# A half-split weight load, batch 1's key features by halves of heads, and a later w2 load in a fused attention and mixer kernel

## The chip, the cores and the metric

The kernel runs on one core of a Trainium2 chip. A core has five engines that matter here: TensorE (PE in the profile, with its weight loads as PEld), VectorE (DVE), ScalarE (ACT), GpSimd (POOL) and SyncE (SP). SP and POOL issue the transfers between the device memory and the on-chip memory; sixteen DMA engines carry them. The metric is the device time of one execution in microseconds (us), and a kernel's time is the median of several executions. Before the change it is 319.8 us, the median of 5 runs (318.88 to 320.85).

## The reference

Eight batches of eight heads, 576 positions, head size 64. The first part is a linear attention with cosine weights, the second a mixer with a low-rank mix over positions and a wide layer over channels:

```python
q_p = phi(q, cos_w, sin_w)          # relu(x)*cos next to relu(x)*sin: 128 features
k_p = phi(k, cos_w, sin_w)
kv  = einsum('bhsf,bhsd->bhfd', k_p, v)
z   = k_p.sum(axis=2)
x   = (q_p @ kv) / (q_p @ z + 1e-6)  # heads side by side: [8, 576, 512]
u   = x + (x^T @ U @ V)^T            # rank 32, over positions
out = u + relu(u @ w_ch1) @ w_ch2    # 512 -> 2048 -> 512
```

The weights `w_ch1` and `w_ch2` are 4 MB each in float32. Inputs and output are float32; the kernel multiplies in bf16.

## The kernel before, in words

**Tiles.** A batch's 576 positions are five chunks: c = 0 to 3 with 128 positions each, and a tail, c = 4, with 64, which lies in the lower or upper half of the partitions for even or odd batches. `kst`, `vst`, `qst` hold a batch's main rows as loaded, `kt`, `vt`, `qt` its tails. `k_prep` and `q_prep` make features from them, one instruction for the cosine half and one for the sine half of a chunk, each on the engine that the call names (lines 228 and 230). `v_prep` and `v_block` cast v into `v_ext` (lines 103 and 105), whose 65th column is one, so that `kv_unit` (line 262) gives kv and z together, for four heads at a time. `kv_unit` runs over five chunks for each of its heads and then casts its result from the accumulator to `kv_sb`. `den_unit` (line 321) makes the denominators and `xh_unit` (line 338) the quotient x for four heads. `A_unit` and the `uTd_` functions make the low-rank part and u transposed. `g1_main` (line 491) makes 128 of the 2048 hidden columns of a batch, with four matmuls, one for each 128 rows of w1 (d = 0 to 3), and a ReLU on ACT (line 500). `g2_part` (line 543) is the second wide layer. `keep_warm` (line 179) issues matmuls on zeros, whose result nobody reads.

**Order.** The order on each engine is written out by hand: the program's order of calls is each engine's order. The first two batches have code of their own: `chain0` and `chain1`. The rest run beside the wide layers, from a plan by slots. A slot is one `g1_main`, `g1_tail` or `g2_part`; what `at(j, ...)` names runs behind slot j of the first batch's wide layer. `chain1` runs behind slot 7. Of batch 0's wide layer, columns j = 0 to 7 come before it, and j = 8 to 13 are spread through it by `fill`, starting with `g1_main(0, 8)` in `fill(1)`.

**The start.** SP issues batch 0's loads in the order q, k, tails, v, and then k and v for heads 4 to 7. POOL issues the weights, casting to bf16 on the way. To hold them back, POOL first copies one element of `vst` into `mark` (line 738), and so waits for v of heads 0 to 3; then comes w1's first quarter of columns (line 91), which j = 0 to 3 need. The second quarter, for j = 4 to 7, is issued inside `chain0`, behind POOL's casts of v for heads 4 to 7. The third and fourth quarters follow a copy that waits for `q_tlT` (line 772). w2, four loads of 512 KB as bf16 (line 97), is issued in slot 6.

`g1_main(0, j, True)` makes only the matmuls d = 0 and 1 and leaves the accumulator open. The program does so for j = 0, then closes the last two quarters of u transposed, and does j = 1 and 2 in the same way, before slot 0 finishes j = 0:

```python
chain_end(0, a0)
g1_main(0, 0, True)
uTd_close(0, 2, V_)
uTd_close(0, 3, A_)
g1_main(0, 1, True)
g1_main(0, 2, True)
```

**Batch 1.** Its q, k, v loads are issued on SP in this order behind `chain0`. Its q buffers are shared with batch 0's, so SP waits there for batch 0's last q features. Slots 4 to 6 make the key features of batch 1, for all eight heads at once, cosine on DVE and sine on ACT, between the ReLUs of j = 4 to 6. `chain1` then starts with `kv_unit(1, 0)`, heads 0 to 3; its cast is on DVE. Behind it come v's cast for heads 4 to 7 on ACT, and further down `kv_unit(1, 1)` for heads 4 to 7, with its cast on ACT. At the end of `chain1`'s first half SP writes one element of the denominators to `mark2` (line 707), and through that wait holds batch 2's loads back, which are issued behind slots 11 and 12. Batch 2's features start in slot 26.

Of the kernel before, what the change touches and what calls it, by code (L numbers as in the profile page):

```python
# [17 lines left out]
def kernel(  # L18
# [18 lines left out]
    P = 128  # L37
# [5 lines left out]
    TS = 64  # L43
# [5 lines left out]
    def tail(b):  # L49
        lo = TS * (b % 2)  # L50
        return slice(lo, lo + TS)
# [34 lines left out]
    w1_bf = const.tile([P, 4, DH], BF16)  # L86
    w2_bf = const.tile([P, NJ, DM], BF16)

    def w1_load(n):
        cs = slice(n * 512, n * 512 + 512)  # L90
        nc.gpsimd.dma_start(
            out=w1_bf[:, :, cs], in_=moe_w_ch1.rearrange("(d p) n -> p d n", p=P)[:, :, cs]
        )

    def w2_load(n):
        js = slice(n * 4, n * 4 + 4)
        nc.gpsimd.dma_start(
            out=w2_bf[:, js, :], in_=moe_w_ch2.rearrange("(j p) n -> p j n", p=P)[:, js, :]
        )

    def cast(eng, o, i):
        if eng is nc.scalar:
            nc.scalar.activation(out=o, in_=i, func=AF.Copy, bias=0.0, scale=1.0)  # L103
        else:
            eng.tensor_copy(out=o, in_=i)  # L105


    V_, A_, G_ = nc.vector, nc.scalar, nc.gpsimd
# [5 lines left out]
        out=iota[:, 0:4], pattern=[[1, 4]], base=0, channel_multiplier=4,  # L114
        allow_small_or_imprecise_dtypes=True,
    )
    for lo in (0, TS):
        nc.gpsimd.iota(
            out=iota[lo : lo + TS, 4:5], pattern=[[1, 1]], base=512, channel_multiplier=1,
# [40 lines left out]
        out=U_bf[:, 0:4, :], in_=moe_U[0:512, :].rearrange("(p c) r -> p c r", c=4)  # L160
# [20 lines left out]
    mark = const.tile([TS, 1], FP32)  # L181
# [16 lines left out]
    def V_evac(eng):  # L198
        cast(
            eng, V_bf.rearrange("p c t -> p (c t)"),  # L200
            v4_ps[0].rearrange("p a n -> p (a n)")[:, 0 : 5 * P],
        )


    k_p, q_p, q_pT, kv_sb, x_bf, A_sb = {}, {}, {}, {}, {}, {}
# [13 lines left out]
    def v_block(b, h0, h1, c0, c1, eng):  # L219
        cast(  # L220
            eng,
            v_ext[b % 2][:, c0:c1, h0:h1, 0:D].rearrange("p c h d -> p h c d"),
            vst[b][:, h0:h1, c0:c1, :],
        )
# [9 lines left out]
    def prep(dst, src, b, c, engs, h0, h1):  # L234
        rows = slice(0, P) if c < 4 else tail(b)
        for i, (w, eng) in enumerate(zip((cosw, sinw), engs)):
            if eng is not None:
                scaled_relu(
                    eng, dst[rows, h0:h1, i * D : i * D + D], src[rows], w[rows, c : c + 1]
                )  # L240

    def k_prep(b, c, engs, h0=0, h1=H):
        if b not in k_p:
            k_p[b] = pool.tile([P, 4, H, 2 * D], BF16, tag="k_p", bufs=1, name="k_p")
        src = kst[b][:, h0:h1, c, :] if c < 4 else kt[b][:, h0:h1, :]
        prep(k_p[b][:, c] if c < 4 else k_tl, src, b, c, engs, h0, h1)
# [7 lines left out]
    def kv_unit(b, hg, tag, bufs, eng=None):  # L254
        if b not in kv_sb:
            kv_sb[b] = pool.tile([P, H, E], BF16, tag="kv", bufs=2, name="kv")
        acc = ps.tile([P, 4, E], FP32, tag=tag, bufs=bufs, name="kv_ps")
        vx = v_ext[b % 2]
        for i in range(4):
            h = hg * 4 + i  # L260
            for c in range(5):
                nc.tensor.matmul(  # L262
                    out=acc[:, i, :],
                    lhsT=k_p[b][:, c, h, :] if c < 4 else k_tl[:, h, :],
                    rhs=vx[:, c, h, :],
                    start=(c == 0),
                    stop=(c == 4),
                )
        cast(eng or V_, kv_sb[b][:, hg * 4 : hg * 4 + 4, :], acc)
# [32 lines left out]
    def qT_of(b, c, h):  # L302
        return q_pT[b][:, c, h, :] if c < 4 else q_tlT[:, h, :]

    def x_alloc(b):
        if b not in x_bf:
            x_bf[b] = pool.tile([P, 4, DM], BF16, tag="x_bf", bufs=2, name="x_bf")

    def x_of(b, c, rows=slice(0, P)):
        return x_bf[b][:, c, :] if c < 4 else x_tl[rows, :]  # L310
# [21 lines left out]
    def xh_unit(b, c, h0, h1, rec, tag, bufs, eng=None):  # L332
        x_alloc(b)
        n = h1 - h0
        rows = slice(0, P) if c < 4 else tail(b)
        acc = ps.tile([P, n, D], FP32, tag=tag, bufs=bufs, name="xh_ps")
        for h in range(h0, h1):
            nc.tensor.matmul(  # L338
                out=acc[:, h - h0, :], lhsT=qT_of(b, c, h), rhs=kv_sb[b][:, h, 0:D],
                start=True, stop=True,  # L340
            )
        if eng is not None:
            for h in range(h0, h1):
                eng.activation(
                    out=x_of(b, c, rows)[:, h * D : h * D + D], in_=acc[rows, h - h0, :],
                    func=AF.Copy, bias=0.0, scale=rec[rows, c, h - h0 : h - h0 + 1],
                )
            return
        nc.vector.tensor_tensor(
            out=x_of(b, c, rows)[:, h0 * D : h1 * D].rearrange("p (i d) -> p i d", d=D),  # L350
            in0=acc[rows],
            in1=rec[rows, c, :].unsqueeze(2).to_broadcast([P if c < 4 else TS, n, D]),
            op=ALU.mult,
        )
# [232 lines left out]
    ORD = (4, 0, 1, 2, 3)  # L587
# [57 lines left out]
    O2, G3 = ("o", 2), ("g", 3)  # L645
# [11 lines left out]
    def chain0():  # L657
        v_prep(0, 0, 4, (4,), (A_,))
        v_block(0, 0, 4, 0, 3, V_)
        v_block(0, 0, 4, 3, 4, A_)  # L660
        k_prep(0, 4, (A_, A_), 4, 8)
        kv_unit(0, 0, "T", 1)
        qtr_unit(0, 4, 0, H, V_, *G3)
        keep_warm(2, "o", 2)
        for c in (0, 1):
            k_prep(0, c, (V_, A_), 4, 8)
        rec0 = den_unit(0, 0, 4, "X", 1)
        for c in (2, 3):
            k_prep(0, c, (V_, A_), 4, 8)
        v_prep(0, 4, 8, (4,), (G_,))  # L670
        v_block(0, 4, 8, 0, 2, G_)
        v_block(0, 4, 8, 2, 4, A_)
        w1_load(1)
        for n, c in enumerate(TL):
            xh_unit(0, c, 0, 4, rec0, *(O2, O2, G3, G3, G3)[n], A_ if n == 1 else None)
        keep_warm(1, "X", 1)
        kv_unit(0, 1, "T", 1, A_)
        rec1 = den_unit(0, 4, 8, "X", 1)
        a0 = A_unit(0, "T", 1, A_, 0, 256)
        for n, c in enumerate(TL[:3]):  # L680
            xh_unit(0, c, 4, 8, rec1, *(O2, O2, G3)[n])
        chain_begin(0)
        uTd_mm(0, 0)
        uTd_mm(0, 1)
        for n, c in enumerate(TL[3:]):
            xh_unit(0, c, 4, 8, rec1, *G3)
        uTd_evac(0, 0, A_)
        uTd_evac(0, 1, A_)
        keep_warm(2, "o", 2)
        return a0  # L690

    def chain1(fill):
        kv_unit(1, 0, "T", 1)
        fill(0)
        rec0 = den_unit(1, 0, 4, "X", 1)
        v_block(1, 4, 8, 0, 4, A_)
        fill(1)
        for n, c in enumerate(ORD):
            xh_unit(1, c, 0, 4, rec0, *O2)
            if n == 1:  # L700
                fill(2)
            if n == 3:
                kv_unit(1, 1, "T", 1, A_)
        fill(3)
        rec1 = den_unit(1, 4, 8, "T", 1)

        nc.sync.dma_start(out=mark2, in_=rec1[0:1, 0, 0:1])
        for c in ORD[:2]:
            xh_unit(1, c, 4, 8, rec1, *O2)
        chain_begin(1)  # L710
        a0 = A_unit(1, "T", 1, A_, 0, 256)
        for c in ORD[2:4]:
            xh_unit(1, c, 4, 8, rec1, *O2)
        fill(4)
        uTd_mm(1, 0)
        uTd_mm(1, 1)
        uTd_evac(1, 0, A_)
        uTd_evac(1, 1, A_)
        xh_unit(1, ORD[4], 4, 8, rec1, *O2)
        fill(5)  # L720
        chain_end(1, a0)
# [7 lines left out]
        if c in (1, 3):  # L729
            keep_warm(1, "X", 1)  # L730
    V_four("X", 1)
    V_evac(V_)
    for c in TL:
        k_prep(0, c, (V_, A_ if c < 3 else V_), 0, 4)
    q_prep(0, 4, (V_, A_))
    keep_warm(14, "o", 2)

    G_.tensor_copy(out=mark, in_=vst[0][0:TS, 0, 0, 0:1])
    w1_load(0)
    a0 = chain0()  # L740
    alloc_q(1)
    load_main(qst[1], q, 1)
# [20 lines left out]
    def at(j, *thunks):  # L763
        beside.setdefault(j, []).extend(thunks)

    for n, c in enumerate(ORD):
        if n > 1:
            at(n - 2, lambda c=c, n=n: q_prep(1, c, (V_, A_ if n % 2 == 0 else V_)))
        tg = ("T", 1) if n % 2 else O2
        at(1 + n, lambda c=c, tg=tg: qtr_unit(1, c, eng=V_, tag=tg[0], bufs=tg[1]))  # L770
        at((4, 5, 5, 6, 6)[n], lambda c=c, n=n: k_prep(1, c, (V_, A_)))
    at(2, lambda: G_.tensor_copy(out=mark, in_=q_tlT[0:TS, 0, TS : TS + 1]))
    at(2, lambda: [w1_load(2), w1_load(3)])
    at(2, lambda: v_prep(1, 0, H, (4,), (G_,)))
    at(2, lambda: v_block(1, 0, 4, 0, 4, G_))
    at(6, lambda: [w2_load(n) for n in range(4)])
    def fill1(n):
        if n in (0, 4):
            u_unit(0, 4 if n == 0 else 0, *(O2 if n == 0 else G3))
# [67 lines left out]
```

## Time and profile before

| | before |
|---|---|
| median of 5 runs | 319.8 us (318.88 to 320.85) |
| the profiled execution | 321.33 us |
| its span, first to last instruction | 319.2 us |
| TensorE clock, mean granted | 0.995 |
| PE busy | 310.9 us (97%) |
| DVE busy | 155.9 us (49%) |
| ACT busy | 151.4 us (47%) |
| POOL busy | 35.2 us (11%) |
| w1 and w2: eight loads of 512 KB on POOL | 9.7 us to landing (median) |

The profile is one execution, recorded by the hardware. A row such as `L491 PE MATMUL g_ps<-uT,w_bf` names the line of the kernel, the engine, the operation and what it writes and reads; the bracket at the end of a row says how long the engine was idle before it and what ended the wait. The chain of work that ended last is followed back from the last instruction, at each step to what released it. Rows of stages give, for each stretch of time, the busy time of each engine with the number of instructions, the share of full speed at which TensorE's clock ran, and the DMA engines' share and rate. In them, PE busy is a modelled time: its matmuls overlap.

### The profile page before, as it was taken

The numbers are of one execution on the slowest core, as the hardware profiler recorded it, in microseconds if no ns is written. First come the engines' busy times: TensorE is split into PE (matmuls) and PEld (weight loads), VectorE is DVE, ScalarE is ACT, GpSimd is POOL, SyncE is SP. The second block draws the span as 40 slices with busy tenths as digits, with TensorE's granted clock in tenths as the row PEclk, the third lists the DMA queues.
The fourth block names the chain that finished last, engine by engine and source line by source line (L and its number), as shares of the span: only waits on it lengthen the run. The fifth ranks groups of instructions, "written<-read, shape, count | busy, mean of one in ns | idle before, by whom it ended". The sixth has DMA issues, their size and how long they took to land.

```text
span 319.2 us, 5795 instructions
## 1 busy us (share of the span) xinstructions
PE 310.9 (97%) x2380; PEld 162.8 (51%) x2380; DVE 155.9 (49%) x355; ACT 151.4 (47%) x261; POOL 35.2 (11%) x67
## 2 busy tenths in 40 slices
PE   8989899999999999999999999999999999999996
PEld 3545464476545544475455444564454444464443
DVE  8768553762877645036926585154836520001211
ACT  5838555685905256658400077559400166650000
POOL 4213400200120140000211100000121100000000
PEclk9999799999999999999999999999999999999999
DMA  8999999946185927970799459900693130001122
GB/s 230 321 256 262 200 217 330 327 134 228 48 216 146 327 74 159 245 241 2 177 252 326 169 121 228 354 10 31 139 174 101 59 91 0 2 0 68 66 87 78
DMA packets 83803, 51.82 MB, mean 162 GB/s; under 512 B 52066, under 2 KB 81026, under 8 KB 83778
## 3 DMA queue, kind: packets, MB, share of 16 engines
q1 hardware_dynamic: 76850, 40.05, 47.0%
q0 software_dynamic: 6784, 11.35, 14.7%
q8 instruction: 18, 0.29, 0.4%
q10 hardware_dynamic: 144, 0.07, 0.1%
q14 instruction: 7, 0.06, 0.1%
HBM read 36.86 MB, written 9.44 MB: 145 GB/s over the span
## 4 chain that ended last, share of the span: by engine, by line
PE 88%; DMA 6%; ACT 4%; SPq 1%; DVE 1%; issue 0%; POOL 0%; DVEq 0%; ACTq 0%
PE o_ps L543 39%; PE g_ps L491 33%; PE gt_ps L511 4%; DMA w_bf<-in_moe_w_ch_dram 3%; PE kv_ps L262 3%; PE va_ps L407 3%; PE x_ps L363 3%; DMA vst<-in_v_dram 2%; ACT hid L500 1%; PE a_ps L390 1%; PE t_ps L279 1%; ACT k_p L228 1%; ACT q_p L228 1%; SPq L81 1%; SPq L75 0%; PE xh_ps L338 0%
## 5 line engine op out<-in xcount | busy, mean ns | idle before, releaser
L500 ACT ACTIVATE hid<-g_ps 128x512 bf16<-128x512 f32 x128 | 76.2, 596 | 102.6 <-PE g_ps L491 102.2
L491 PE MATMUL g_ps<-uT,w_bf 128*128 128x512 bf16 x512 | 120.0, 382 | 0.9 <-DMA w_bf<-in_moe_w_ch_dram 0.9
L543 PE MATMUL o_ps<-w_bf,hid 128*128 128x512 bf16 (+2 forms) x528 | 119.2, 373 | 0.0
L491 PEld LDWEIGHTS <-w_bf 128*128 128x128 bf16 x512 | 49.0, 98 | 57.5 <-DMA w_bf<-in_moe_w_ch_dram 1.3
L543 PEld LDWEIGHTS <-hid 128*128 128x128 bf16 x528 | 48.7, 98 | 52.8 <-issue 1.7
L553 DVE TENSOR_TENSOR o_sb<-u_bf,o_ps 128x512 f32<-128x512 bf16 (+2 forms) x33 | 22.1, 668 | 62.7 <-PE o_ps L543 62.6
L563 POOL DMA_DIRECT2D out_dram<-o_sb x24 | 13.5, 561 | 165.8 <-DVE o_sb L553 155.8
L408 DVE TENSOR_TENSOR u_bf<-x_bf,va_ps 128x512 bf16<-128x512 bf16 x32 | 21.8, 685 | 10.1 <-PE va_ps L407 10.1
L105 DVE CAST kv<-kv_ps 128x260 bf16<-128x260 f32 x14 | 6.0, 429 | 32.0 <-PE kv_ps L262 32.0
L373 DVE TENSOR_TENSOR x_bf<-x_ps,rec 128x512 bf16<-128x512 f32 x24 | 16.6, 691 | 0.8
L228 ACT ACTIVATE q_p<-qst,sinw 128x512 bf16<-128x512 f32 (+1 forms) x24 | 15.1, 658 | 2.2 <-DMA qst<-in_q_dram 2.1
L511 PE MATMUL gt_ps<-uT_tl,w_bf 128*128 128x128 bf16 x256 | 15.6, 219 | 0.0
L407 PE MATMUL va_ps<-A_sb,V_bf 128*128 128x512 bf16 x40 | 15.2, 379 | 0.0
L543 PE MATMUL o_ps<-w_bf,hid_tl 128*128 128x512 bf16 x64 | 15.1, 379 | 0.0
L511 PEld LDWEIGHTS <-w_bf 128*128 128x128 bf16 x256 | 14.6, 98 | 0.5
L313 DVE TENSOR_SCALAR rec<-x_ps 128x8 f32<-128x8 f32 (+1 forms) x30 | 4.9, 165 | 20.2 <-PE x_ps L363 20.1
L262 PEld LDWEIGHTS <-k_p 128*128 128x128 bf16 x256 | 11.5, 97 | 5.8 <-ACT k_p L228 1.5
L230 DVE TENSOR_SCALAR k_p<-kst,cosw 128x512 bf16<-128x512 f32 (+1 forms) x31 | 14.3, 482 | 0.0
L262 PE MATMUL kv_ps<-v_ext,k_p 128*128 128x65 bf16 x256 | 12.4, 193 | 1.6 <-ACT k_p L228 0.9
L179 PE MATMUL w_ps<-zero 128*128 128x512 bf16 x35 | 11.1, 457 | 1.2 <-DVE U_bf L162 1.2
L518 ACT ACTIVATE hid_tl<-gt_ps 128x512 bf16<-128x512 f32 x16 | 9.4, 597 | 5.5 <-PE gt_ps L511 5.5
L103 ACT ACTIVATE v_ext<-vst 128x512 bf16<-128x512 f32 (+2 forms) x19 | 11.8, 636 | 0.5 <-DMA vst<-in_v_dram 0.4
(106 smaller groups left out, 252.6 us busy)
## 6 DMA issues: line engine op xcount, KB each, us to landing
qst<-in_q_dram SPq DMA_DIRECT2D x7, 1024.0 KB, 9.1
kst<-in_k_dram SPq DMA_DIRECT2D x7, 1024.0 KB, 8.1
vst<-in_v_dram SPq DMA_DIRECT2D x6, 1024.0 KB, 8.2
out_dram<-o_sb POOLq DMA_DIRECT2D x24, 256.0 KB, 2.9
w_bf<-in_moe_w_ch_dram POOLq DMA_DIRECT2D x8, 512.0 KB, 9.7
vst<-in_v_dram SPq DMA_DIRECT2D x4, 512.0 KB, 8.6
out_dram<-o_sb SPq DMA_DIRECT2D x7, 256.0 KB, 2.3
qst<-in_q_dram SPq DMA_DIRECT2D x2, 512.0 KB, 3.7
```

Source lines behind the costliest of these rows:

```text
L228: nc.scalar.activation(out=o, in_=i, func=AF.Relu, bias=0.0, scale=w)
L230: eng.tensor_scalar(out=o, in0=i, scalar1=0.0, scalar2=w, op0=ALU.max, op1=ALU.mult)
L262: nc.tensor.matmul(out=acc[:, i, :], lhsT=k_p[b][:, c, h, :] if c < 4 else k_tl[:, h, :], rhs=vx[:, c, h, :], start=(c == 0), stop=(c == 4),)
L373: nc.vector.tensor_tensor(out=x_of(b, c, rows).rearrange("p (g i d) -> p g i d", g=2, d=D), in0=view[:, :, :, 0:D], in1=rec[rows].unsqueez ...
L407: nc.tensor.matmul(out=va, lhsT=V_bf[:, c, :], rhs=A_sb[b], start=True, stop=True)
L408: nc.vector.tensor_tensor(out=u_bf[b][:, c, :] if c < 4 else u_tl[b // 2][rows, :], in0=x_of(b, c, rows), in1=va[rows, :], op=ALU.add,)
L491: nc.tensor.matmul(out=g_ps.rearrange("p (c t) -> p c t", c=4), lhsT=w1_bf[:, d, j * P : j * P + P], rhs=uT[b][:, :, d, :], start=(d == 0) ...
L500: nc.scalar.activation(out=hid[b][:, j, :], in_=g_ps, func=AF.Relu, bias=0.0, scale=1.0)
L511: nc.tensor.matmul(out=g_ps[:, jj, :], lhsT=w1_bf[:, d, j * P : j * P + P], rhs=uT_tl[pr][:, d, :], start=(d == 0), stop=(d == 3),)
L543: nc.tensor.matmul(out=o[:, cols], lhsT=lhs[:, j, c * P : c * P + P], rhs=w2_bf[:, j, cols], start=(j == 0), stop=(j == NJ - 1),)
L553: nc.vector.tensor_tensor(out=o_sb[:, cols], in0=u[:, cols], in1=o[:, cols], op=ALU.add)
L563: eng.dma_start(out=out[b, 0:512, cols].rearrange("(p c) n -> p c n", c=4)[:, c, :], in_=o_sb[:, cols],)
```

## The change

Five edits:

1. `w1_load` takes a range of 128-row blocks. The first quarter of columns is loaded as two transfers, rows of d = 0 and 1 first, d = 2 and 3 behind. Both are on POOL, one after the other.
2. w2's four loads leave slot 6. They are issued in `chain1`, behind a POOL copy that reads one element of `kv_sb[1]`, and so waits for the cast of `kv_unit(1, 0)`.
3. Batch 1's key features in slots 4 to 6 are made for heads 0 to 3 only. Those of heads 4 to 7 move into `chain1`: cosine on DVE for chunks 4, 0, 1 ahead of `kv_unit(1, 0)`, and for chunks 2, 3 behind `den_unit(1, 0..4)`; sine on ACT, all five, behind `kv_unit(1, 0)`. v's cast for heads 4 to 7 moves from behind the denominators to behind these five.
4. `V_evac`, the DVE copy of the replicated V from its accumulator, moves from ahead of batch 0's key features to behind DVE's cast of v in `chain0`.
5. In `chain0`, x of chunk 1 for heads 4 to 7 is made by four ACT instructions and not by one DVE instruction.

```diff
-    def w1_load(n):
+    def w1_load(n, d0=0, d1=4):
         cs = slice(n * 512, n * 512 + 512)
         nc.gpsimd.dma_start(
-            out=w1_bf[:, :, cs], in_=moe_w_ch1.rearrange("(d p) n -> p d n", p=P)[:, :, cs]
+            out=w1_bf[:, d0:d1, cs],
+            in_=moe_w_ch1.rearrange("(d p) n -> p d n", p=P)[:, d0:d1, cs],
         )
...
     def chain0():
         v_prep(0, 0, 4, (4,), (A_,))
         v_block(0, 0, 4, 0, 3, V_)
+        V_evac(V_)
...
-            xh_unit(0, c, 4, 8, rec1, *(O2, O2, G3)[n])
+            xh_unit(0, c, 4, 8, rec1, *(O2, O2, G3)[n], A_ if n == 1 else None)
...
     def chain1(fill):
+        for c in ORD[:3]:
+            k_prep(1, c, (V_, None), 4, 8)
         kv_unit(1, 0, "T", 1)
+        G_.tensor_copy(out=mark, in_=kv_sb[1][0:TS, 0, 0:1])
+        for n in range(4):
+            w2_load(n)
+        for c in ORD:
+            k_prep(1, c, (None, A_), 4, 8)
+        v_block(1, 4, 8, 0, 4, A_)
         fill(0)
         rec0 = den_unit(1, 0, 4, "X", 1)
-        v_block(1, 4, 8, 0, 4, A_)
+        for c in ORD[3:]:
+            k_prep(1, c, (V_, None), 4, 8)
         fill(1)
...
     V_four("X", 1)
-    V_evac(V_)
...
-    w1_load(0)
+    w1_load(0, 0, 2)
+    w1_load(0, 2, 4)
...
-        at((4, 5, 5, 6, 6)[n], lambda c=c, n=n: k_prep(1, c, (V_, A_)))
+        at((4, 5, 5, 6, 6)[n], lambda c=c: k_prep(1, c, (V_, A_), 0, 4))
...
-    at(6, lambda: [w2_load(n) for n in range(4)])
```

`ORD` is (4, 0, 1, 2, 3); `V_`, `A_`, `G_` are DVE, ACT and POOL.

## The prediction

> **What bounds the kernel now.** I read the page first: PE is busy 310.9 of 319.2 us and nothing else is over half. So time can only be won where PE stands idle or runs slowly, and the waits of PE say where: 0.9 us for a w1 transfer, 0.9 us for the key features (line 228), the rest in the first 19 us. All lie before 37 us, so I read the chain of waits there, in order of time (start, length, what):
>
> ```profile
> 12.70 0.52 POOL mark L738
> 13.21 9.72 DMA w_bf<-in_moe_w_ch_dram
> 22.98 0.61 PE g_ps L491 x2
> ...
> 28.38 1.05 PE g_ps L491 x4
> 29.46 0.60 ACT hid L500
> 30.08 0.72 ACT k_tl L228
> 30.82 0.60 ACT hid L500
> 31.44 1.33 ACT k_p L228 x2
> 32.78 0.48 ACT hid L500
> 33.26 1.23 ACT k_p L228 x2
> 34.53 0.70 PE kv_ps L262 x17
> 35.26 0.44 DVE kv L105
> ```
>
> Two things set the pace: w1's first quarter until 22.98, and ACT from 29.46, which alternates ReLUs with sine features until kv of batch 1 can run. Between them PE's weight loads show something that the chain hides:
>
> ```profile
> 22.98 0.11 PEld L491 LDWEIGHTS <-w_bf 128*128 128x128 bf16 x2 [1.12 <-DMA w_bf<-in_moe_w_ch_dram]
> ...
> 28.38 0.55 PEld L491 LDWEIGHTS <-w_bf 128*128 128x128 bf16 x4 [0.17 <-DMA w_bf<-in_moe_w_ch_dram]
> ```
>
> The second row is j = 4, the first user of w1's second quarter. That transfer was issued at 16.25 and took 12.1 us (the tile's answer for its issue), so it landed at 28.35: PE met it with hardly any slack. The rows of stages show what follows kv's wait:
>
> ```profile
> 33.00:34.00 1.00, 0.44 (x5) 0.23 (x3) 1.00 (x3) 1.00 (x3) 1.00 (x2) 1.00 1.25 209
> 34.00:35.00 1.00, 0.61 (x16) 0.49 (x17) 0.33 (x1) 1.00 (x3) 1.00 (x3) 1.00 1.25 209
> 35.00:36.00 1.00, 0.69 (x20) 0.41 (x17) 0.74 (x2) 0.93 (x1) 0.59 (x1) 1.00 1.07 154
> 36.00:37.00 1.00, 1.00 (x19) 0.59 (x16) 0.73 (x3) 0.00 (x0) 0.00 (x0) 0.76 1.23 201
> 37.00:38.00 1.00, 1.00 (x10) 0.49 (x8) 0.00 (x0) 0.10 (x1) 0.00 (x0) 0.50 1.23 199
> ```
>
> PE is 0.44 to 0.69 busy for three microseconds, then its clock (third number from the end) is 0.50 until 39.9. Four matmuls of j = 8 take 1.62 us instead of 1.03. That slow stretch is 3.4 us long and costs half of it, 1.7 us.
>
> **What the Trainium skill says.** (1) "TensorE: Matmul & The Clock Gate", Part 1: the clock falls to half when a free-running window of 3413 ns was idle, so where the window lies differs from run to run. The length agrees (36.5 to 39.9); the stretch before it was not idle, only thin, so the trace shows a wider condition. (2) "DMA: Bandwidth & Descriptors", Anatomy of one DMA: about 2 us of a POOL transfer are fixed, mostly the wait for the last byte's receipt. It agrees: the POOL queue, read by windows, has moved the first quarter's 0.52 MB by about 21.1 (packets start at 16.8, then 0.12 MB per us), and the landing is at 22.93. (3) "SBUF — State Buffer", Who interferes with whom: a DVE feature instruction with both sides in SBUF and a POOL instruction exclude each other. It agrees: of batch 1's cosine instructions, 0.47 us each, the one that meets POOL's v cast (31.50 to 32.54) takes 1.30.
>
> **Edit 1, the split.** One POOL issue more: 0.77 us, at 13.98 to 14.75. Behind it POOL casts v's tail at 14.76 and waits for v's rows until 15.68, so the second quarter is still issued at 16.25. Half of the bytes are moved at 18.8; with the same 1.9 us of receipt the first half lands at 20.7. PE is free for it at 22.03 (the end of line 442's eight matmuls), so it starts 0.95 us earlier. The second half lands where the whole did, at 22.98 to 23.3 (bounds: nothing, and a quarter microsecond if SP's loads take more of the engines). It is needed after eight matmuls of 0.216 us, at 23.76. Covered by 0.5 us; without this cover each microsecond is paid in full. But then PE reaches j = 4 at 27.43, and the second quarter, behind the same bytes in the same queue, still lands at 28.35. PE waits there for 0.95 us. Net: 0. Bounds: −0.3 if the second quarter comes early (batch 1's k tail, issued at 14.53 and 15.3 us on the way, then holds ACT instead), +0.3 if it is later by the second transfer's overhead.
>
> **Edit 3, the halves.** ACT's sine instruction takes 0.72 us for 512 columns and 0.49 for 256 (0.43 from start to start in batch 0's features). From the chain: first ReLU ends 30.06; tail half to 30.5; j = 5's matmuls end 30.73, so its ReLU ends 31.36; two halves to 32.2; ReLU to 32.75; two halves to 33.6. Before, the last ended at 34.48. kv's last 17 matmuls start 0.9 us earlier. v is no obstacle: POOL's cast ends at 32.54. DVE has three half cosines (0.27 from start to start) ahead of kv's cast: its own h 0..4 features end near 33.1, so it is free at 33.95, and kv's matmuls end at 34.3. Hidden; if DVE were late the cast would slip by the same. **−0.9.**
>
> What ACT gets back is 5 × 0.43 = 2.2 us of sines ahead of v's cast (1.07 us). Before, the ACT rows are:
>
> ```profile
> 34.86 1.07 ACT L103 ACTIVATE v_ext<-vst 128x1024 bf16<-128x1024 f32 x1
> 37.90 0.60 ACT L500 ACTIVATE hid<-g_ps 128x512 bf16<-128x512 f32 x1 [1.97 <-PE g_ps L491]
> ```
>
> so 2 us were idle there. Now: ReLU of j = 7 to 34.05, sines to 36.2, v's cast to 37.2, then the ReLU of j = 8. Queued behind are the ReLUs of j = 8 and 9; three accumulators let PE go on without them. kv for heads 4 to 7 needs v's cast: PE comes there (0.43 kv cast, 0.64 denominators, j = 8 and 9 with 0.86 each, x) at about 37.5. Covered by 0.3; bounds 0 and +0.4. On DVE the two half cosines behind the denominators end at 36.5, when the first x is wanted. 0.
>
> **The clock.** With kv 0.9 us earlier and then 0.9 us of full PE work inside the same stretch, PE's thin stretch shrinks from 3.07 (33.17 to 36.24) to 2.1 us, shorter than the 3.4 us of the slow stretch. I count the slow clock as gone: 1.7 us in this execution. Whether the timed runs had it the trace can't say: their spread, 2.0 us, is about its size. Bounds 0 and −1.7; I take 0.7 of it, because the one execution seen had it. **−1.2.**
>
> **Edit 2, w2.** POOL waits for kv's cast at 34.76; behind it on POOL are only the w2 issues and batch 2's v casts, which waited until 53.26 for data. Issue at 35.1, packets 2.6 us later as for w1's third quarter. Its 2.1 MB at the 0.205 MB per us of the rows above take 10.2 us. First use at 71.57: hidden by over 20 us. But SP's loads of batch 2 (43.70 on, 3.5 MB at 0.33) now start up to 2.6 us earlier and overlap it: 37.7 + 10.2 + 10.7 + 2 = 60.6 for the last, q, which before landed at 51.23 + 8.5 = 59.7. ACT reads it first at 63.89 − 2.6 = 61.3. Covered by 0.7; bounds 0 and +1. **0.**
>
> **Edits 4 and 5.** V's copy (0.82 us) goes into DVE's idle 0.85 us ahead of kv's cast at 14.09. The features before it end earlier, but v lands at 12.65 anyway. SP's q tail for batch 1 (12.74, waiting for these features) leaves 0.7 us earlier with k and v behind it; that is the +0.25 above. Four ACT instructions (0.90 us) fit between 19.31 and 20.29, where ACT was idle 0.98. x's tail on DVE still ends near 21.16, since PE makes it late. Both 0, bounds ±0.2.
>
> **Sum.** In the profiled execution (span 319.2, 2.1 around it, 321.33): −0.9 − 1.7 = 318.7. The median stands 1.5 below that execution, so I use the weighted clock: 319.8 − 0.9 − 1.2 = **317.7 us**.
>
> **Rivals.** *The clock stays as it was, or the timed runs never had it*: 319.8 − 0.9 = 318.9. For it: the window moves freely. Against: the thin stretch is a third shorter. *The split pays*: the second quarter also lands earlier, −0.3 more: 317.3. Against: it follows the same bytes. *A late transfer gives it back*: w1's third quarter landed at 35.2, and j = 8 now wants it at 35.3; or batch 2's q, or v's cast, each up to 1 us: 319.3. *Slower*: w1's second quarter, behind two transfers, comes later than 28.35. Each microsecond delays j = 4, the ReLUs, the sines and kv. From 3.7 us late (2.1 gained, 1.6 for half a per cent) it decides, at 321.5; POOL's 0.9 us of slack ahead of its issue speaks against it.
>
> **Numbers.** First forecast 0.55 (317.0 to 318.5), clock rival 0.2, split 0.08, late transfer 0.1, slower 0.07. Half a per cent, 1.6 us, is about what a measurement can tell from no change: below 318.2 is faster. That gives faster 0.57 (most of the first case and the split), slower 0.07, same 0.36. The range, 316.8 to 319.4, leaves out the slower case and some of the edges.
>
> **What would show it.** PE's first w1 matmul near 22.0; a wait for w1 at j = 4, near 27.4 to 28.4; kv's last matmuls from 33.6; no clock below 1.0 near 37; w2 issues near 35; no PE wait at 37.5 or 61. It is wrong if j = 4 doesn't wait, if the clock still falls, or if ACT's sines hold kv of heads 4 to 7.

## The result, and the profile after

| | before | after |
|---|---|---|
| median | 320.08 us (79 runs, 317.99 to 323.65) | 319.48 us (44 runs, 317.21 to 322.49) |
| ratio, 95% interval | | 0.998 (0.9966 to 0.9993) |
| the profiled execution | 321.33 us | 318.45 us |
| its span | 319.2 us | 316.7 us |
| TensorE clock in it, mean granted | 0.995 | 1.0 |

The ratios here leave out disturbed runs, so they are not exactly quotients of the medians. The change gains 0.6 us, a fifth of a per cent. The interval of the ratio ends below 1, but the gain is less than the half per cent that the prediction took for the least that a measurement can tell, and under a third of the forecast. The two profiled executions, though, differ by 2.9 us. The forecast for the profiled execution was 318.7, and 318.45 came; the forecast for the median was 317.7, and 319.48 came. So the trace should show the predicted steps nearly all in place, and it does; part of that agreement is luck, as is said further down.

The chain of waits of after (start, length, what):

```profile
16.16 11.54 DMA w_bf<-in_moe_w_ch_dram
...
27.75 1.04 PE g_ps L492 x4
...
30.14 0.61 ACT hid L501
30.76 0.91 ACT k_p L229 x2
31.66 0.48 ACT hid L501
32.15 0.80 ACT k_p L229 x2
...
33.00 0.70 PE kv_ps L263 x17
33.72 0.44 DVE kv L106
...
52.13 9.06 DMA qst<-in_q_dram
61.25 0.05 issue
61.30 0.72 ACT q_p L229
```

Each pair of half sines takes 0.80 to 0.91 us where the whole ones took 1.23 to 1.33, and kv's last 17 matmuls start at 33.00 instead of 34.53. 0.63 of these 1.53 us come from j = 4, which started at 27.75 instead of 28.38; 0.90 come from the halves. The stretch of the chain shown here begins with w1's second quarter, and behind it the chain has a new link: batch 2's q, at 61.

PE's weight loads of after (start, length, what; the bracket is the idle time before and what ended it):

```profile
21.73 0.15 PEld L492 LDWEIGHTS <-w_bf 128*128 128x128 bf16 x2
...
27.75 0.55 PEld L492 LDWEIGHTS <-w_bf 128*128 128x128 bf16 x4 [0.74 <-DMA w_bf<-in_moe_w_ch_dram]
...
32.99 0.10 PEld L263 LDWEIGHTS <-k_p 128*128 128x128 bf16 x1 [0.30 <-ACT k_p L229]
```

The first w1 matmul no longer waits (22.98 before, 21.73 now), and j = 4 waits 0.74 us for the second quarter: more than half of the 1.25 us won at the start is lost six microseconds on. The wait for k is down to 0.30.

The rows of stages of after (PE, PEld, DVE, ACT, POOL busy; the third number from the end is TensorE's clock):

```profile
33.00:34.00 1.00, 0.90 (x18) 0.62 (x19) 0.28 (x1) 0.97 (x3) 0.00 (x0) 1.00 1.22 203
34.00:35.00 1.00, 0.80 (x22) 0.68 (x22) 0.86 (x3) 1.00 (x3) 0.73 (x2) 1.00 1.22 209
35.00:36.00 1.00, 1.00 (x13) 0.55 (x12) 0.96 (x4) 1.00 (x3) 1.00 (x3) 1.00 0.65 89
36.00:37.00 1.00, 0.96 (x8) 0.48 (x7) 0.91 (x4) 1.00 (x3) 1.00 (x2) 1.00 0.94 53
```

PE is 0.80 busy at the least, where before it was 0.44 to 0.69, and the clock stays at 1.00. ACT, which idled 2 us there, is full: its rows of after are

```profile
33.95 1.71 ACT L229 ACTIVATE k_p<-kst,sinw 128x256 bf16<-128x256 f32 x4
35.56 1.06 ACT L104 ACTIVATE v_ext<-vst 128x1024 bf16<-128x1024 f32 x1
36.53 1.04 ACT L501 ACTIVATE hid<-g_ps 128x512 bf16<-128x512 f32 x2
```

v's cast ends at 36.6, before kv for heads 4 to 7 starts on PE at 37.14.

### The profile page after: what moved, and what is told of

Its sections match the earlier page's. It is cut to its first block, busy times and chain, and to the rows that moved or that the text cites. A ratio compares the mean times of both kernels' runs of the same rounds, so it can differ in the third digit from the quotient of the medians.

```text
span 316.7 us, 5813 instructions
## 1 busy us (share of the span) xinstructions
PE 309.5 (98%) x2380; PEld 162.5 (51%) x2380; DVE 156.2 (49%) x359; ACT 153.5 (48%) x270; POOL 36.5 (12%) x69
## 4 chain that ended last, share of the span: by engine, by line
PE 80%; DMA 8%; SPq 6%; ACT 2%; DVE 1%; issue 1%; POOL 0%; DVEq 0%; ACTq 0%
PE o_ps L544 39%; PE g_ps L492 27%; PE gt_ps L512 4%; SPq L81 4%; DMA w_bf<-in_moe_w_ch_dram 4%; DMA qst<-in_q_dram 3%; PE kv_ps L263 3%; PE x_ps L364 3%; SPq L75 2%; PE va_ps L408 2%; DMA vst<-in_v_dram 2%; PE a_ps L391 1%; ACT hid L501 1%; ACT q_p L229 1%; PE t_ps L280 1%; ACT k_p L229 1%
## 5 line engine op out<-in xcount | busy, mean ns | idle before, releaser
L492 PE MATMUL g_ps<-uT,w_bf 128*128 128x512 bf16 x512 | 118.5, 379 | 0.6 <-DMA w_bf<-in_moe_w_ch_dram 0.6
L229 ACT ACTIVATE k_p<-kst,sinw 128x256 bf16<-128x256 f32 (+1 forms) x23 | 11.9, 570 | 0.3 <-DMA kst<-in_k_dram 0.3
```

Source lines behind the costliest of these rows:

```text
L229: nc.scalar.activation(out=o, in_=i, func=AF.Relu, bias=0.0, scale=w)
L492: nc.tensor.matmul(out=g_ps.rearrange("p (c t) -> p c t", c=4), lhsT=w1_bf[:, d, j * P : j * P + P], rhs=uT[b][:, :, d, :], start=(d == 0) ...
```

## The experiments

The question was where two thirds of the forecast went. The theories: (A) the path got shorter as predicted, but the slow stretch of the clock, worth 1.2 us in the sum, was rarer before than I took it to be, or isn't gone after; (B) something behind kv gives the gain back, w2's move and batch 2's late q first of all; (C) the gain is that of the split and not of the halves.

**How the runs are read.** Each execution reports its mean granted TensorE clock. One stretch of 3.4 us at half speed in a span of 317 us makes 0.995; so an execution at 0.997 or more had no slow stretch ("full clock"). The table puts together all runs of a kernel; before's 257 are those that ran on the same chips as the four sets of experiments. Errors are standard errors; the means of two sets of the same kernel differed by up to 0.5 us, so single sets can't settle less. The full-clock runs of a kernel are those that happened to keep the clock. Where half of the runs lost it, the rest may be the ones with the shorter waits, and their mean may flatter the kernel; that is a possibility, not something shown.

| kernel | runs | mean, us | at full clock, us | with a slow stretch |
|---|---|---|---|---|
| before | 257 | 320.20 ± 0.08 | 319.58 ± 0.06 | 35% (they average 321.3) |
| after | 88 | 319.42 ± 0.12 | 319.04 ± 0.11 | 22% (they average 320.8) |
| edit 3 alone | 14 | 318.89 ± 0.24 | 318.59 ± 0.15 | 14% |
| after, w2 back in slot 6 | 58 | 319.06 ± 0.14 | 318.80 ± 0.12 | 14% |
| edits 2 and 3 | 22 | 319.45 ± 0.26 | 319.01 ± 0.22 | 23% |
| after without edit 3 | 22 | 320.11 ± 0.28 | 319.16 ± 0.19 | 45% |
| edit 1 alone | 14 | 320.11 ± 0.31 | 319.21 ± 0.16 | 50% |
| edits 4 and 5 | 22 | 320.61 ± 0.35 | 319.42 ± 0.24 | 50% |
| before, with more filler | 22 | 319.87 ± 0.18 | 319.87 ± 0.18 | none |

### Which edit gains: the halves alone, and all but the halves

Edit 3 put alone into before, and after with edit 3 undone:

```diff
     def chain1(fill):
+        for c in ORD[:3]:
+            k_prep(1, c, (V_, None), 4, 8)
         kv_unit(1, 0, "T", 1)
+        for c in ORD:
+            k_prep(1, c, (None, A_), 4, 8)
+        v_block(1, 4, 8, 0, 4, A_)
...
-        v_block(1, 4, 8, 0, 4, A_)
+        for c in ORD[3:]:
+            k_prep(1, c, (V_, None), 4, 8)
...
-        at((4, 5, 5, 6, 6)[n], lambda c=c, n=n: k_prep(1, c, (V_, A_)))
+        at((4, 5, 5, 6, 6)[n], lambda c=c: k_prep(1, c, (V_, A_), 0, 4))
```

> The kernel before with edit 3 alone: batch 1's key features by halves of heads, w2 still in slot 6, w1's first quarter whole. Theory A (the halves give 0.9 us on the path, and w2's move gives part of it back because batch 2's q lands too late): 1.0 to 1.6 us under the kernel before, so more than the whole change gives (0.6), and in the trace kv's last matmuls near 33.6, batch 2's q landing before 60. Theory B (the halves give nothing in most runs, the loads of k and v set kv): within 0.3 us of the kernel before. Theory C (the clock alone makes the difference): the mean clock of the runs rises and runs of equal clock agree with the kernel before.

> The changed kernel with edit 3 undone: key features of all eight heads in slots 4 to 6, as before; w2 still behind kv, the split and edits 4 and 5 kept. Theory A: the gain of the halves goes, so 0.0 to 0.4 us over the kernel before; kv's last matmuls near 34.5. Theory B (edit 3 gives nothing): as the changed kernel, 0.6 us under the kernel before.

Alone: 318.68 us (14 runs), ratio 0.9973 (0.9952 to 0.9994). Undone: 320.15 us (22 runs), 0.9995 (0.9973 to 1.0018). So over all runs the gain goes with the halves, and (C) falls: without them the other four edits leave 0.09 ± 0.29 us in the mean. At full clock the halves alone give 319.58 − 318.59 = 0.99 ± 0.16 us, where the prediction had 0.9. PE's weight loads with edit 3 alone:

```profile
22.91 0.11 PEld L491 LDWEIGHTS <-w_bf 128*128 128x128 bf16 x2 [1.04 <-DMA w_bf<-in_moe_w_ch_dram]
...
33.38 0.10 PEld L262 LDWEIGHTS <-k_p 128*128 128x128 bf16 x1 [0.30 <-ACT k_p L228]
```

The wait for w1 at 22.91 is untouched and the last wait for k is 0.30, as in after. With whole features the thin stretch is back, in the stages of after without edit 3:

```profile
32.00:33.00 1.00, 0.47 (x3) 0.10 (x1) 1.00 (x3) 1.00 (x3) 0.73 (x1) 1.00 1.14 246
33.00:34.00 1.00, 0.28 (x2) 0.10 (x1) 0.41 (x2) 1.00 (x2) 0.00 (x0) 1.00 1.18 249
34.00:35.00 1.00, 0.84 (x18) 0.63 (x19) 0.11 (x1) 0.59 (x2) 0.00 (x0) 1.00 1.22 231
35.00:36.00 1.00, 0.70 (x22) 0.60 (x21) 0.90 (x2) 0.08 (x1) 0.56 (x2) 1.00 1.13 189
36.00:37.00 1.00, 1.00 (x5) 0.40 (x3) 0.46 (x2) 1.00 (x1) 1.00 (x2) 0.64 0.29 51
```

and behind it, from 36.3, the slow clock.

At full clock the two tests do not agree. After without edit 3 stands at 319.16 there, 0.42 ± 0.20 us under before, and the halves add only 0.12 ± 0.22 to that; what they add in the mean, 0.69 ± 0.30, is mostly the rarer slow stretches, 22% in place of 45%. Either the twelve runs of that kernel that kept the clock are a favourable choice, or the other edits win part of the same wait that the halves win. The runs don't tell which.

### The split alone

```diff
-    w1_load(0)
+    w1_load(0, 0, 2)
+    w1_load(0, 2, 4)
```

> The kernel before with edit 1 alone, w1's first quarter in two transfers. Theory A (the gain at the first matmul is lost at j = 4, which waits for the second quarter): within 0.2 us of the kernel before; first w1 matmul near 22.0, PE idle about 0.6 to 1 us ahead of j = 4. Theory B (the split pays): 0.5 to 0.9 us under the kernel before, no wait at j = 4. Theory C (the second quarter lands later behind two transfers): over the kernel before by 0.3 us or more.

320.22 us (14 runs), ratio 1.0011 (0.9987 to 1.0036): no gain shown. (Its full-clock mean is 0.37 lower, but from seven runs only; its mean over all runs is lower by 0.09.) PE's weight loads with the split alone:

```profile
21.92 0.15 PEld L492 LDWEIGHTS <-w_bf 128*128 128x128 bf16 x2
...
27.92 0.55 PEld L492 LDWEIGHTS <-w_bf 128*128 128x128 bf16 x4 [0.74 <-DMA w_bf<-in_moe_w_ch_dram]
```

PE starts 1.06 us earlier than before and waits 0.74 at j = 4, which still starts 0.46 earlier. The rest is lost on ACT, which now waits for batch 1's k tail, where before it came to it without a wait:

```profile
30.23 0.72 ACT L229 ACTIVATE k_tl<-kt,sinw 64x512 bf16<-64x512 f32 x1 [0.63 <-DMA kt<-in_k_dram]
```

kv's last matmuls start at 34.68, against 34.53 before. The same wait, 0.73 us, stands in the profile of after without edit 3. In other executions with the split the second quarter came early enough. PE's weight loads of after with w2 in slot 6, in the first of its profiles:

```profile
26.48 0.59 PEld L492 LDWEIGHTS <-w_bf 128*128 128x128 bf16 x4
...
31.93 0.23 PEld L263 LDWEIGHTS <-k_p 128*128 128x128 bf16 x2 [0.73 <-ACT k_p L229]
32.46 0.10 PEld L263 LDWEIGHTS <-k_p 128*128 128x128 bf16 x1 [0.30 <-ACT k_p L229]
```

There j = 4 has no wait; ACT waits 0.88 us for batch 1's k tail, and PE then waits for k, 1.03 us in all. In these executions the microsecond won at the start is spent, for the most part, in front of one of these transfers or features.

### Edits 4 and 5 alone

```diff
         v_block(0, 0, 4, 0, 3, V_)
+        V_evac(V_)
...
-            xh_unit(0, c, 4, 8, rec1, *(O2, O2, G3)[n])
+            xh_unit(0, c, 4, 8, rec1, *(O2, O2, G3)[n], A_ if n == 1 else None)
```

> The kernel before with edits 4 and 5 alone: V's copy behind v's cast, x of chunk 1 for heads 4 to 7 on ACT. Both are in engines' idle times, so within 0.2 us of the kernel before at full clock (319.56), and a slow stretch in a third of the runs. Rival: DVE's earlier features let SP issue batch 1's loads earlier, which delays or hastens w1's second quarter: 0.3 us or more off.

320.19 us (22 runs), 1.0006 (0.9982 to 1.003): no difference shown, as predicted; the full-clock mean is 0.16 ± 0.25 under before's.

### The clock: filler matmuls in the thin stretch

Before, with six more matmuls on zeros ahead of `kv_unit(1, 0)`; nothing else is changed:

```diff
-    at(7, lambda: keep_warm(2, "X", 1))
+    at(7, lambda: keep_warm(8, "X", 1))
```

> The kernel before with eight instead of two matmuls on zeros ahead of chain1, which fill 1.3 us of PE's wait for kv's features. Theory A (the thin stretch at kv makes the slow clock): runs with a slow stretch fall from 37% to under 15%, and the mean by 0.3 to 0.6 us; runs at full clock stay within 0.2 us of those of the kernel before. Theory B (the slow clock comes from elsewhere): the share stays above 30% and the time within 0.2 us.

319.9 us (22 runs), ratio 0.998 (0.9958 to 1.0002). None of the 22 runs has a slow stretch, against 35% of before's. The stages of this kernel:

```profile
33.00:34.00 1.00, 1.00 (x6) 0.49 (x5) 1.00 (x3) 1.00 (x3) 0.33 (x1) 1.00 1.17 247
34.00:35.00 1.00, 0.76 (x5) 0.20 (x2) 1.00 (x1) 1.00 (x3) 1.00 (x2) 1.00 1.16 246
35.00:36.00 1.00, 1.00 (x21) 0.82 (x21) 0.16 (x1) 0.74 (x2) 1.00 (x2) 1.00 1.15 252
36.00:37.00 1.00, 0.70 (x21) 0.47 (x19) 0.96 (x2) 0.00 (x0) 1.00 (x2) 1.00 0.82 136
```

At 35%, none in 22 would come by chance about once in ten thousand times. So the thin stretch at kv is what lets the clock fall in nearly all of these runs of before, and this one edit shows it. But the filler seems to cost 0.29 ± 0.19 us at full clock, where 0.2 at most was expected, and the whole nets 0.33 ± 0.20. A slow stretch costs 321.32 − 319.58 = 1.74 us, but only in a third of the runs: 0.6 us of before's mean. That is half of the 1.2 that the forecast counted.

Filler with the halves, two more matmuls ahead of `kv_unit` and one more ahead of `den_unit`, and after with w2 in slot 6 and two more matmuls ahead of `kv_unit`:

```diff
         fill(0)
+        keep_warm(1, "X", 1)
         rec0 = den_unit(1, 0, 4, "X", 1)
...
-    at(7, lambda: keep_warm(2, "X", 1))
+    at(7, lambda: keep_warm(4, "X", 1))
```

(the line ahead of `den_unit` in the first of the two only).

> Edit 3 alone, with four instead of two matmuls on zeros ahead of chain1 and one more ahead of the denominators of heads 0 to 3. Theory A (halves 0.97 us at full clock, and the slow clock is what the thin stretch costs): no slow stretch in over 90% of the runs, 1.2 to 1.6 us under the kernel before, about 318.6. Theory B: the added matmuls delay kv, and the time is that of edit 3 alone or 0.2 to 0.4 us more.

> The changed kernel with w2 in slot 6 and four instead of two matmuls on zeros ahead of chain1: the candidate for a version better than both. If the slow clock comes from the thin stretch at kv: at most 1 run in 10 with a slow stretch, and the mean 1.3 to 1.6 us under the kernel before. If the added matmuls delay kv: full-clock mean 0.2 to 0.4 us over that of the same kernel without them.

318.86 us, 0.9978 (0.9956 to 1.0001), and 319.39 us, 0.9976 (0.9957 to 0.9995), 22 runs each. The share of slow stretches, 9% in both, can't be told from the 14% of the same kernels without filler, and the full-clock means, 319.16 and 319.25, are some 0.5 higher. The means are 0.75 and 0.89 under before's, where 1.2 to 1.6 were expected: no gain of the filler beside the halves is shown.

### The same kernel again

After unedited, in two more sets:

> The changed kernel once more, unedited, as the measure for the others of this set. So far the kernel before ran without a slow clock stretch in 37 of 59 runs, and the changed kernel in 33 of 44. If the clock is not what the change moves, again a quarter of the runs has a slow stretch, and the median is 0.5 to 0.7 us under the kernel before.

> The changed kernel once more, on the same chip as the others of this set. Full-clock mean 318.9 to 319.1, 0.4 to 0.6 us under the kernel before; a slow stretch in about a fifth of the runs.

318.89 us, 0.9965 (0.9941 to 0.9989), and 319.71 us, 0.9969 (0.9948 to 0.999), 22 runs each. The second one's profiled execution has a slow stretch, in another place. Its stages:

```profile
16.00:17.00 1.00, 0.35 (x9) 0.26 (x8) 1.00 (x4) 0.98 (x4) 0.95 (x2) 1.00 1.01 335
17.00:18.00 1.00, 0.54 (x18) 0.45 (x15) 0.52 (x2) 0.85 (x4) 0.39 (x1) 1.00 1.19 320
...
19.00:20.00 1.00, 1.00 (x17) 1.00 (x18) 0.89 (x3) 0.87 (x4) 0.00 (x0) 0.51 1.16 239
20.00:21.00 1.00, 1.00 (x8) 0.64 (x6) 0.15 (x1) 0.44 (x3) 0.00 (x0) 0.50 1.19 242
```

This is batch 0's chain, where the halves change nothing. (Edits 1, 4 and 5 do, but the share of runs with a slow stretch is the same without them: 7 of 36 with the halves and without these edits, 27 of 146 with the halves and these edits.) The profiled executions fall in line: each of the four with whole features and no added filler (before, edit 1 alone, edits 4 and 5 alone, after without edit 3) has its slow stretch between 36 and 42. Of the eleven with the halves and w2 no later than in after, seven have none, two (both with w2 in slot 6) have it between 35 and 39, and two between 19 and 24. In the two at kv, ACT had waited 0.88 and 0.78 us for batch 1's k tail. All runs of these kernels, those with added filler left out: with whole features 119 of 315 have a slow stretch (38%), with the halves 39 of 204 (19%). The halves make the clock's fall rarer, and leave other places to it.

The clock is not the only thing that changes from run to run. One execution of the kernel with w2 in slot 6 (see below; the profile of its second set) took 321.07 us without a slow stretch: batch 1's v landed late,

```profile
34.69 1.04 POOL L106 CAST v_ext<-vst 128x1024 bf16<-128x1024 f32 x1 [2.26 <-DMA vst<-in_v_dram]
```

and PE waited 2.0 us for this cast ahead of kv.

### w2's move: back to slot 6, and later still

After with edit 2 undone, three times:

```diff
     at(2, lambda: v_block(1, 0, 4, 0, 4, G_))
+    at(6, lambda: [w2_load(n) for n in range(4)])
...
         kv_unit(1, 0, "T", 1)
-        G_.tensor_copy(out=mark, in_=kv_sb[1][0:TS, 0, 0:1])
-        for n in range(4):
-            w2_load(n)
```

> The changed kernel with w2 issued in slot 6 again (edit 2 undone). Theory A (w2 behind kv overlaps batch 2's loads, and ACT waits for q near 61): 0.4 to 0.9 us under the changed kernel, 1.0 to 1.5 under the kernel before; q of batch 2 lands near 58 to 59 and ACT doesn't wait for it. Theory B (the move of w2 is hidden): as the changed kernel, 0.6 us under the kernel before.

> The changed kernel with w2 in slot 6, unedited from the first set, beside the others on one chip. Theory A (w2's move costs about 0.4): full-clock mean 318.6 to 318.9 again, slow stretch in about a fifth of the runs. Theory B: about 319.0, as the changed kernel has it.

> The changed kernel with w2 in slot 6, on the same chip as the changed kernel. Theory A (w2's move costs 0.3 to 0.4 us): full-clock mean 318.6 to 318.8, and 0.2 to 0.5 us under the changed kernel of this set. Theory B (scatter): within 0.15 us of it.

and edits 2 and 3 together in before:

> The kernel before with edits 3 and 2: features by halves, and w2 behind kv; w1's first quarter whole, edits 4 and 5 left out. So far runs at full clock: kernel before 319.56 (77 runs), edit 3 alone 318.59 (12), changed kernel 319.02 (52). Theory A (w2's move takes back about 0.4 us): full-clock mean 318.9 to 319.2. Theory B (it takes back nothing, and the changed kernel's weaker gain is scatter): 318.4 to 318.7.

With w2 in slot 6: 318.85 us (22 runs), 0.9966 (0.9945 to 0.9987); 318.63 (14), 0.9969 (0.9942 to 0.9996); 319.06 (22), 0.9954 (0.9932 to 0.9975). Edits 2 and 3: 319.35 (22), 0.9988 (0.9968 to 1.0007). Put together, the kernels with the halves and w2 in slot 6 (72 runs, edit 3 alone among them) average 319.03 ± 0.12, those with the halves and w2 behind kv (110 runs) 319.43 ± 0.11. The move takes back 0.40 ± 0.16 us, of which 0.28 ± 0.14 at full clock: two to two and a half standard errors. No single set shows it by itself.

Does more of the same do more? w2 behind batch 1's second x chunk (36.97 in the trace of after, some 2.8 us later), and behind the denominators for heads 4 to 7 (near 40.0, 5.8 us later):

```diff
             if n == 1:
+                G_.tensor_copy(out=mark, in_=x_bf[1][0:TS, 0, 0:1])
+                for m in range(4):
+                    w2_load(m)
                 fill(2)
```

```diff
         rec1 = den_unit(1, 4, 8, "T", 1)
+        G_.tensor_copy(out=mark, in_=rec1[0:TS, 0, 0:1])
+        for n in range(4):
+            w2_load(n)
```

> The changed kernel with w2 about 2.8 us later: POOL's copy waits for x of chunk 4's neighbour, chunk 0, heads 0 to 3, and not for the cast of kv. Theory A: q of batch 2 lands near 63, ACT waits 1 to 2 us, and the kernel is 1.2 to 2.2 us over the changed kernel. Theory B: within 0.4 us of it.

> The changed kernel with w2 held back further: POOL's copy waits for the reciprocals of heads 4 to 7 and not for the cast of kv, so about 5.5 us later. Theory A (w2 delays batch 2's q, which ACT waits for near 61): the delay grows, q lands near 65 (42.3 for w2's first packet, 10.2 + 10.7 + 2 us), ACT waits 3 to 4 us and the kernel is 2.5 to 4 us over the changed kernel. Theory B (w2's place costs nothing by that way): within 0.5 us of the changed kernel.

2.8 us later: 322.05 us (19 runs), 1.0064 (1.0042 to 1.0087); at full clock 321.76 ± 0.19, 2.7 above after, where 1.2 to 2.2 were expected. 5.8 us later: 327.63 us (6 runs), 1.0203 (1.0151 to 1.0254), some 8 us above after, where 2.5 to 4 were expected. ACT's waits in the two, from 50 to 85 us of the first

```profile
ACT q_p L229 <- DMA qst<-in_q_dram: 1.8, 1, 1.8
...
ACT q_tl L229 <- DMA qt<-in_q_dram: 1.1, 1, 1.1
```

and from 55 to 75 us of the second (us in total, times, longest):

```profile
ACT q_tl L229 <- DMA qt<-in_q_dram: 4.0, 1, 4.0
ACT q_p L229 <- DMA qst<-in_q_dram: 2.2, 1, 2.2
```

say how: batch 2's q lands late (issued at 53.85 in the first, 52.13 in after), and the ReLUs are queued behind its sine features on ACT, so PE stops. PE's rows of the first:

```profile
60.87 1.02 PE L492 MATMUL g_ps<-uT,w_bf 128*128 128x512 bf16 x4 [0.40 <-ACT hid L501]
63.88 1.02 PE L492 MATMUL g_ps<-uT,w_bf 128*128 128x512 bf16 x4 [1.99 <-ACT hid L501]
```

Together they are 2.4 us, near the 2.7 of the mean. (The execution itself took 320.72, the second fastest of the 19, so its total doesn't show the cost: it was 1.2 us ahead of after's until this wait, and it has a slow stretch of its own behind it, from 65.0 to 68.4.) In the second kernel PE's stops are longer, 3.29 and 1.54 us, and all six of its runs have slow stretches; in its profiled execution, the slowest of the six, the clock is low for about 10 us behind the first stop (rows of stages, 68.6 to 78.8). So with w2 2.8 us later the cost is, in the mean, nearly a microsecond for each microsecond, in the place that the prediction named.

### Is it q in the change itself

After, with batch 2's loads in the order k, q, v instead of k, v, q:

```diff
-    for n, t in enumerate(loads(2, nc.sync)):
+    kk, vv, qq = loads(2, nc.sync)
+    for n, t in enumerate((kk, qq, vv)):
         put((11, 12, 12)[n], t)
```

> The changed kernel with batch 2's loads in the order k, q, v instead of k, v, q: w2 stays behind kv, but q lands some 2.5 us earlier, near 58, and ACT can't wait for it. Theory A (w2's place costs 0.36 us at full clock because q then lands too late in many runs): full-clock mean 318.5 to 318.8, as with w2 in slot 6. Theory B (the cost is not by way of q, or is scatter): as the changed kernel beside it, within 0.2 us.

319.3 us (22 runs), 0.9967 (0.9945 to 0.9988); full clock 319.01 ± 0.18, against 319.04 for after. q is issued at 47.6 and lands 11.6 later, at 59.2, 3.8 us before ACT reads it:

```profile
63.08 0.71 ACT L229 ACTIVATE q_p<-qst,sinw 128x512 bf16<-128x512 f32 x1
```

while ACT's row of after is

```profile
61.30 0.72 ACT L229 ACTIVATE q_p<-qst,sinw 128x512 bf16<-128x512 f32 x1 [0.19 <-DMA qst<-in_q_dram]
```

and PE waits for ACT a little later:

```profile
66.33 0.61 PE L280 MATMUL t_ps<-ident,q_p 128*128 128x128 bf16 x8 [0.40 <-ACT q_tlT L104]
```

Of these 0.40 us q's lateness can account for 0.19 at most. With q safe no gain is seen, 0.03 ± 0.21 us; the error is too wide to exclude the 0.28. So (B) holds for a later w2, but the 0.28 us that the change's own move costs are not shown to go by way of q. In the other profiled executions with the halves and w2 behind kv, q landed 0.4 to 1.2 us ahead of its use. Whether another transfer of these microseconds costs it, or part of it is scatter, stays open.

## Why the prediction was wrong

**The step that failed is "The clock".** It counted −1.2 us, as 0.7 of 1.7. The size of one slow stretch was right: 1.74 us. Both shares were wrong. I weighted it with 0.7 because the one profiled execution had it, and then took all of that as removed. In fact 35% of before's runs have a slow stretch and 22% of after's: (0.354 − 0.216) × 1.74 = 0.24 us, where 1.2 was counted. Before's mean held only 0.35 × 1.74 = 0.6 us of it, so 0.6 of the 1.2 was never there to be won; and 0.22 × 1.75 = 0.4 is still in after's, part of it in batch 0's chain, of which the prediction said nothing. The figures shown could have told the first: the profiled execution, 321.33, stood above the highest of the five runs, 320.85. An execution above them all, by about a slow stretch from their median, is a sign that the stretch is not the rule. The prediction read the same gap ("the median stands 1.5 below that execution") and yet gave the stretch 0.7.

**The path, −0.9: right for the halves alone.** They give 0.99 ± 0.16 us at full clock, and all kernels with the halves and w2 in slot 6 together 0.82 ± 0.12. All five edits give 319.58 − 319.04 = 0.54. Of the 0.45 that this falls short of the halves alone, w2's move accounts for 0.28 ± 0.14; the rest is within the scatter. Beside the other four edits the halves show only 0.12 ± 0.22 at full clock, so how the 0.54 is shared among the edits is not settled. So the sum for the mean is −0.54 − 0.24 = −0.78, which is 320.20 − 319.42; the forecast had −2.1. Of the 1.3 us missing, 0.96 are the clock and 0.36 the path.

**The profiled execution, 318.7: right with some luck.** Before's profile was a typical run with a slow stretch (they average 321.3), and after's was better than a typical run at full clock, 318.45 against 319.04; w1's early second quarter alone gave it 0.63 us. So the two profiles differ by 2.9 us where the means differ by 0.8.

**Edit 2, "covered by 0.7; 0": its cover was too thin.** q's landing was put at 60.6 and came at 61.2 in the profiled execution; its need was put at 61.3 and came at 61.1. ACT waited 0.19. The bounds, 0 and +1, hold the 0.28 to 0.40 measured, and the rival "a late transfer gives it back" is true in part, though q isn't shown to be the transfer. Another one that it named was late at times: w1's third quarter held PE's weight loads for 0.15 to 0.59 us at j = 8 in five of the thirteen profiled executions with the halves. The limit was in the right place all the same: with w2 another 2.8 us later, nearly each microsecond is paid.

**The split, 0: right in the mean, with one bound too narrow.** First matmul 21.73 (forecast 22.0), wait at j = 4 until 27.75, by 0.74 (forecast 0.95). But j = 4 came 0.63 us earlier than in before's execution, and 0.46 earlier with the split alone: up to twice the bound of 0.3 for an early second quarter. What then took the gain back with the split alone is the wait that the prediction set beside this bound, batch 1's k tail holding ACT. Over all runs of the split alone no gain is left; the full-clock mean, 0.37 ± 0.17 lower from seven runs, leaves a small one possible.

**Edit 3's covers, and edits 4 and 5: right.** v's cast (forecast to end at 37.2, came at 36.6) didn't hold kv for heads 4 to 7, and w2 was issued at 34.45 (forecast 35.1). Edits 4 and 5 alone show no difference. "v is no obstacle" held in before's and after's executions, but not in all: in the one of 321.07 us kv waited 2.0 us for v.

**The rivals.** "The clock stays as it was, or the timed runs never had it" forecast 318.9. It is the nearest in kind, and was given 0.2. Each of its parts is half true: the clock stayed in part, and most of the timed runs never had the stretch. The slower rival had no part: in none of the profiled executions did w1's second quarter come 3.7 us late; the longest wait for it was 1.6 us. Three of the rivals' figures don't follow from their terms: the split's is 317.4 and not 317.3, the slower one's limit 321.4 and not 321.5, and no sum that is given leads to 319.3 for the late transfer. Nothing above rests on them.

**The version that follows from the runs** is the change without edit 2: 319.03 us in the mean over 72 runs (edit 3 alone among them), 1.2 below before and 0.4 below after.

## What to carry to other kernels

A profile is one execution: before a cost in it goes into a sum, ask how many executions have it, and set the profiled time against the timed runs; one that stands above all of them holds something that most of them lack. A term that occurs by chance is entered as share before minus share after, times its size, and the share after is not zero because one place was filled while other thin places remain. A mean over the runs that kept the clock is a mean over chosen runs, and is read beside the mean over all. A transfer covered by less than the scatter of its own landing (here from 0.2 us late to 1.2 early) is not covered, and what it then costs is read from the queue behind the instruction that waits for it.

## What the runs showed of the hardware

In these runs TensorE's clock falls to half for 3.4 us after stretches in which PE was only thin, not idle: 0.44 to 0.69 busy for three microseconds before it, 0.35 and 0.54 for two in batch 0's chain. The Trainium skill, "TensorE: Matmul & The Clock Gate", Part 1, tells of an idle window of about this length, and of one kernel whose clock swings because PE idles briefly between groups of matmuls. These runs agree with the length; their thin stretches are nearer to the second case. The fall is a matter of chance, in 35% of the runs of one and the same program, and six filler matmuls brought it to 0 of 22. And a 2.8 us later issue of w2 cost 2.7 us in the mean, although w2 itself isn't needed until 69: the cost comes by way of batch 2's q, which was issued and landed later.
